# Partial sums kept in PSUM, a fifth chunk in seven products, and two output stages in seven

## The chip, the cores and the metric

One NeuronCore of a Trainium2 chip. TensorE (PE) multiplies into PSUM, VectorE (DVE) and ScalarE (ACT) read PSUM and SBUF, GpSimd (POOL) works on SBUF, SyncE (SP) issues DMAs. The metric is the device time of one execution in microseconds, here the median of three runs.

## The reference

A linear attention with 8 batches of 8 heads, 576 tokens of 64 features, followed by a feed-forward layer whose hidden value is the largest of three products.

```python
def phi(x):
    proj = np.einsum('bhsd,df->bhsf', x, w_phi)               # 64 -> 128
    proj = proj - np.max(np.abs(proj), axis=-1, keepdims=True)
    return np.concatenate([np.exp(proj), np.exp(-proj)], axis=-1)
q_p, k_p = (phi(q), phi(k))
kv = np.einsum('bhsf,bhsd->bhfd', k_p, v)
z = np.sum(k_p, axis=2)
num = np.einsum('bhsf,bhfd->bhsd', q_p, kv)
den = np.einsum('bhsf,bhf->bhs', q_p, z)[..., None] + 1e-06
x = (num / den) transposed to (batch, token, head, feature), reshaped to (4608, 512)
h = np.maximum(np.maximum(x @ w1, x @ w2), x @ w3)            # 512 -> 768
out = h @ w_out                                               # 768 -> 512
```

## The kernel before, in words

The attention is cut into 16 units `u` of four heads of one batch (`attention`). A unit loads and transposes q and k, projects both (`project`), takes maxima on DVE (`reduce`), exponentials on ACT (`k_exp`, `q_exp`), scales v on POOL, sums kv on PE, and then makes numerators: for each of its four heads PE writes two PSUM tiles of 5 x 65 columns, one for exp(proj) and one for exp(-proj) (L683); DVE scales the first into the SBUF tile `y` (L692), adds the second (L695), takes a reciprocal for two heads together (L740), and POOL multiplies it in (L741). A transposing DMA carries the result into `xT`, which holds x turned, per batch.

The feed-forward layer runs in nine chunks (`chunk`): chunks 0 to 7 are the first 512 tokens of a batch each, chunk 8 the last 64 tokens of all eight. With W2 and W3 held as differences from W1, h is W1's product plus the larger of two products clamped at zero; W1's part goes straight to the output by the product `line_w` of W1 and W_out, so that an output tile is four matmuls on x (`straight`, L924) and six on h (`down`, L929). Chunks in `SEVEN` (6, 7, 8) compute their two up products as one 2 x 2 block product with seven block multiplications in place of eight (`seven_products`): sums of quarters of x (`xs`, L799) and of the weights (`ws`, L996) are made ahead by POOL, and for each of three pairs of hidden blocks PE makes seven products of four 256-column matmuls (L820). ACT copies one of them to SBUF (L845) and DVE forms the partial sums by adding PSUM to SBUF (`joined`, L829, seven a pair); then come a relu (L862) and a maximum (L864), two of each a pair. The other chunks take 48 matmuls of 512 columns (L891), with a relu on ACT (L905) or DVE (L907) and a maximum on DVE (L901).

All of a core's work is a list of nodes. A hand-kept table, `PLAN`, gives every node its engine, its place in the order, its buffer slots and a planned start; `plan` reads it, and the instructions are written out in that order, so each engine's queue is fixed. A planned start is read only to order bank filling at the start of the kernel. `buf` and `bank` name slots shared by several tiles: eight PSUM banks, and SBUF tiles such as `raw`, `Ek0`, `Eq1`.

Of the kernel before, what the change touches and what calls it, by code (L numbers as in the profile page):

```python
# [16 lines left out]
DF = 128  # L17
DM = H * D
# [30 lines left out]
YS = 3  # L49
# [4 lines left out]
OSB = 4  # L54
EITHER = 2
SEVEN = (6, 7, 8)
# [3 lines left out]
class Buf:  # L60
# [6 lines left out]
    def __call__(self):  # L67
        if self.tile is None:
            self.tile = self.make(self)
        return self.tile  # L70

# [19 lines left out]
103G0@1.2 3A@0.7 1D@0.8 4A@1.3 10S0@0.7 12D1@4.0 11A@4.0 5D@4.2 0G@1.9 19T0@4.5 20A0@4.9 6D@4.4 29T12@5.5 32D0@6.0 9G@2.5 8G@3.2  # L91
35D@6.6 31A0@6.8 102G@3.9 260G2@4.6 16S0@1.1 104G@8.1 17G@8.3 186G3@8.6 185G@9.3 259G@10.0 1166G@10.7 13S@2.5 7A@7.2 106T3@7.4 33A0@7.5
34A@8.0 30A@8.4 107D1@8.1 119T45@8.8 122D1@9.3 187S1@2.9 124A1@9.2 123A1@9.7 112T67@9.1 115D@9.9 110T0@9.4 111A@10.2 114A@10.6
120A@11.1 121A@11.6 25T2@10.0 15D@10.5 14D@10.7 27T1@10.9 21T3@11.1 118D@10.9 26D@11.5 28D@11.8 43T04@12.2 73T21@12.3 22D@12.0
23T3@12.7 125D@12.4 113A@12.1 46D@13.0 47D0@13.3 18S1@4.3 24D@13.6 116A@12.6 76A0@13.0 45A@13.5 1169G@11.5 54A0@13.8 75A0@14.0
117A@14.4 1167G@12.2 74A@14.9 36T56@13.1 108T4@13.8 42D@14.0 39D@14.6 109D@15.2 38A@15.4 77A@15.9 41A@16.4 58A@16.8 51T37@15.1 52D@15.8
44A@17.0 126T24@15.9 130D1@16.4 105S2@5.0 131T13@16.5 333G1@13.6 129D@16.7 53D@17.0 133D@17.6 57G0@14.3 55G@14.5 2G@15.6 56G@15.8
188G@16.9 128A@17.3 37A@17.6 137A1@18.0 40A@18.2 78T0@17.5 62T47@17.8 80A@18.7 64A0@19.0 132D@18.2 48T35@18.4 50D@18.8 63D@19.4
49D@19.6 60G@17.2 61G@18.3 138G1@18.4 59G@19.5 127A@19.1 79A@19.4 68T67@19.3 134T15@19.6 263T4@19.9 190T3@20.4 135D@20.2 65T20@21.0
71A@19.7 69A@20.2 72A@20.7 70A@21.2 141A@21.6 67A@21.8 139G@20.6 334S0@8.7 142G@22.0 261G@23.1 140G@23.3 81A0@22.0 136D@20.8 191D2@21.4  # L100
264D3@22.0 192T1@21.6 85T76@22.1 86D0@22.6 66A@22.2 193A@22.3 1168G@23.5 82T05@22.4 161T3@22.7 83D@23.0 90T47@23.2 151T21@23.6
163A1@23.2 162A1@23.5 87D@23.4 93T03@23.9 265T6@24.2 84D@23.8 91D1@24.2 94D@24.6 404G0@24.2 88D0@25.1 92D@25.2 145T54@24.8 153A@24.0
155A@24.5 154A@25.0 152A@25.5 146A1@25.9 164A1@26.1 147A@26.3 194T0@25.5 1188T7@25.7 156T12@26.3 195A@26.4 144G@24.4 335G@24.6
337S0@35.1 95D@25.6 266D@26.0 1189D0@26.6 165T54@26.6 168T03@26.9 143G@24.8 166D2@27.1 169D@27.5 148T67@27.3 167D@27.9 96D1@28.4
149D@28.5 170D@28.7 189S3@36.5 1192T5@28.0 158A@26.7 403G@25.9 159A@27.2 157A@27.7 160A@28.1 262S0@42.1 150A@28.6 1190T0@28.4
1191D@29.1 171D2@29.7 1193A@28.8 89G0@26.6 332G@27.8 97G@28.6 301T46@29.0 176T31@29.3 173T27@29.6 1198T0@29.9 177D0@29.9 174D@30.2
178D@30.6 175D@31.1 179D0@31.6 304A0@29.7 305A0@30.1 302A@30.6 303A@31.1 196T53@31.3 1199A@31.6 276T21@31.6 98T7@31.9 402G@29.8
267T6@32.1 100T4@32.3 199D0@31.8 279D1@32.4 101D@33.0 268D@33.4 99D@33.6 172G1@30.6 281A0@32.0 1200T0@32.5 181T4@33.8 197A0@32.5
277A1@33.1 198A1@33.6 1201A@34.1 180G@31.9 203T67@34.2 183T5@34.5 1196T0@34.8 202D@34.0 182D@34.6 206D@35.0 406S1@42.8 338S@45.5
184D@35.6 291T45@36.2 208A@34.6 207A@35.1 278A@35.6 209D@36.0 292D0@36.6 293D@37.2 282D@37.9 204A@36.1 201A@36.6 205A@37.0 200A@37.5  # L110
1194T2@36.5 1195A@38.0 1197A@38.5 1171G@33.6 1172G@35.7 1170G@37.8 210T74@37.9 215T56@38.0 214D1@38.5 216D@38.8 280A@39.0 213D@39.4
1210T3@38.4 1173G@39.9 217D@39.7 1174G@42.0 1175G@44.1 269T20@39.3 288T45@39.5 1211A1@39.5 271A@39.9 270A@40.4 212A@40.9 273A@41.1
211A@41.6 289D@40.3 290D@40.9 274A@41.9 1206T1@40.1 1208T6@40.9 1214T3@41.8 272D@41.5 1207D@42.1 283T74@42.8 228T52@42.9 1215A@42.9
1209D@42.7 275D@43.3 287D@43.9 1204T1@43.2 230A1@43.4 229A1@43.8 1205D@44.3 1212T3@44.1 218T60@45.0 306T45@45.2 231A@44.3 285A@44.8
221A0@45.0 284A@45.2 222G0@46.5 1218T1@45.6 1213D@45.1 220D@45.7 286D@46.3 219D@46.7 1219D@47.3 309A@45.7 224A@46.1 310A@46.3 307A@46.7
294A1@47.2 308A@47.4 232A@47.9 1226T3@46.4 223G@48.5 1227D@47.9 1224T0@47.3 1225D@48.5 233T76@48.2 241A0@48.4 235A@48.7 353T15@48.5
475S1@47.7 1216T4@48.7 357D1@49.1 234A@49.2 339T23@49.6 238T0@49.9 356D0@49.4 1217D@49.8 225T57@50.5 345D@50.4 342D@51.0 236A@49.6
240A@50.2 473S1@48.4 237A@50.4 239A@50.9 346T46@51.6 227A0@51.8 226A@52.1 352D@52.0 349D@52.6 354A0@52.3 355A1@52.6 1220T0@51.9
344A@52.9 343A@53.3 296G1@50.6 242T75@52.8 341A@53.8 407S@49.8 336S2@51.9 612S0@52.5 243D1@53.3 1221D@53.7 340A@54.3 1222T1@53.1
245T37@54.0 253T02@54.9 244D@54.3 246D@54.7 297G@52.6 295G@52.8 472G3@54.8 471G@55.6 474G@56.3 1223D@55.1 254D2@55.7 247D@56.1  # L120
298T53@55.3 351A@54.8 347A@55.2 348A@55.7 350A@56.2 476S2@59.0 542G2@56.5 255D@56.5 415T10@56.5 408T74@56.7 248D1@56.9 300A1@56.7
299A@57.0 418D1@57.0 311T6@56.9 364A0@57.2 313A@57.4 314A1@57.7 312A@57.9 367A0@58.1 420A0@58.2 417A@58.7 250T23@57.1 251D@57.7
# [975 lines left out]
```

## Time and profile before

| | us |
|---|---|
| median of 3 runs | 276.3 (275.75 to 281.68) |
| the profiled execution | 276.54 |
| its span, first to last instruction | 274.7 |
| mean granted clock of TensorE | 0.993 |
| busy: PE, DVE, ACT, POOL | 265.6, 241.5, 214.2, 186.9 |
| instructions | 8748 |

The page of a profile lists busy times, the span in 40 slices with the busy share in tenths, the chain of work that ended last, and groups of instructions with their count, their total busy time and the mean time of one. Matmuls are pipelined, so their single times overlap; the step from one to the next is shorter than the mean of one.

### The profile page before, as it was taken

Reading aid. Unit: us, or ns where it says so; the run is one execution under the profiler, and the core shown is the slowest. Engines: PE = TensorE matmul, PEld = TensorE weight load, DVE = VectorE, ACT = ScalarE, POOL = GpSimd, SP = SyncE. Lnnn points to the kernel's source line nnn. Section 1 sums busy time; section 2 is a strip of 40 time slices with the busy share of each in tenths; the row PEclk is TensorE's granted clock in tenths of the full one; section 3 lists DMA queues with packets and bytes.
Section 4 is the critical chain, followed back from the end, with each engine's and each line's share of the span. In section 5 each row is a group of like instructions: output and inputs, shape, how many; then the busy total and the mean of one; then the engine's idle time right before and its main releaser. Section 6 shows DMA issues by size and latency. Waiting matters only on the chain.

```text
span 274.7 us, 8748 instructions
## 1 busy us (share of the span) xinstructions
PE 265.6 (97%) x3540; PEld 159.8 (58%) x3540; DVE 241.5 (88%) x489; ACT 214.2 (78%) x516; POOL 186.9 (68%) x183
## 2 busy tenths in 40 slices
PE   7789999999999999999999999999999999999994
PEld 4458744566565556565655455655548766686652
DVE  3799999999999888988888998999898999998871
ACT  3999999999999999779878989799987443254241
POOL 6798999999769951987569279937899856600000
PEclk9989999999999999999999999999999999999999
DMA  6999999999999999999999994596505053020253
GB/s 143 258 220 209 210 195 242 249 175 193 193 195 160 262 178 254 212 217 204 180 201 164 240 216 70 108 248 156 128 6 161 2 98 115 0 76 4 47 154 144
DMA packets 76200, 44.54 MB, mean 162 GB/s; under 512 B 52672, under 2 KB 67328, under 8 KB 76160
## 3 DMA queue, kind: packets, MB, share of 16 engines
q1 hardware_dynamic: 60880, 31.93, 53.6%
q0 software_dynamic: 14912, 11.77, 29.1%
q8 instruction: 27, 0.44, 0.6%
q10 hardware_dynamic: 368, 0.30, 0.3%
q14 instruction: 13, 0.11, 0.1%
HBM read 34.64 MB, written 9.44 MB: 160 GB/s over the span
## 4 chain that ended last, share of the span: by engine, by line
PE 89%; DVE 4%; ACT 3%; DMA 2%; issue 0%; POOLq 0%
PE ups L891 21%; PE ops L929 17%; PE ops L924 12%; PE ups L820 10%; PE psn L683 8%; PE kvps L616 7%; PE psm L642 3%; PE psq L545 3%; PE psk L545 3%; DMA qk_bf<-in_k_dram 2%; PE pm L1018 2%; ACT Eq L633 2%; DVE mk L549 2%; PE tps L508 1%; ACT Ek L553 1%; PE pst L545 1%
## 5 line engine op out<-in xcount | busy, mean ns | idle before, releaser
L633 ACT ACTIVATE Eq<-psm 128x512 bf16<-128x512 f32 (+1 forms) x160 | 81.7, 579 | 6.7 <-PE psm L642 6.1
L597 POOL TENSOR_TENSOR vab<-v_raw,em 128x1152 bf16<-128x1152 f32 (+1 forms) x36 | 68.3, 1906 | 17.5 <-ACT em L591 17.4
L553 ACT ACTIVATE Ek<-psk 128x512 bf16<-128x512 f32 x128 | 71.6, 641 | 2.2 <-DVE mk L549 1.2
L891 PE MATMUL ups<-xT,w_bf 128*128 128x512 bf16 x288 | 69.7, 380 | 0.0
L741 POOL TENSOR_TENSOR x_sb<-y,rden 128x640 bf16<-128x640 f32 x32 | 39.7, 1252 | 20.8 <-DVE rden L740 20.1
L929 PE MATMUL ops<-wout_bf,hT 128*128 128x512 bf16 (+2 forms) x222 | 52.0, 374 | 0.0
L549 DVE TENSOR_REDUCE mq<-psq 128x4 f32<-128x512 f32 x64 | 41.2, 681 | 4.8 <-PE psq L545 4.6
L549 DVE TENSOR_REDUCE mk<-psk 128x4 f32<-128x512 f32 x64 | 42.2, 681 | 2.2 <-PE psk L545 1.4
L891 PEld LDWEIGHTS <-w_bf 128*128 128x128 bf16 x288 | 25.0, 98 | 26.3 <-issue 1.3
L692 DVE TENSOR_TENSOR y<-psn,sq 128x325 f32<-128x325 f32 x64 | 30.6, 492 | 3.9 <-PE psn L683 3.1
L929 PEld LDWEIGHTS <-hT 128*128 128x128 bf16 x222 | 20.7, 98 | 21.7 <-DVE hT L864 0.5
L683 PEld LDWEIGHTS <-Eq 128*128 128x128 bf16 x640 | 26.1, 98 | 11.4 <-issue 2.3
L695 DVE TENSOR_TENSOR y<-y,psn 128x325 f32<-128x325 f32 x64 | 30.2, 487 | 2.1
L939 ACT COPY osb<-ops 128x512 f32<-128x512 f32 (+2 forms) x29 | 16.9, 582 | 17.2 <-PE ops L929 16.8
L829 DVE TENSOR_TENSOR parts<-ups,parts 128x512 f32<-128x512 f32 (+1 forms) x45 | 29.1, 679 | 1.1 <-PE ups L820 0.8
L683 PE MATMUL psn<-kv_sb,Eq 128*128 128x65 bf16 x640 | 28.7, 194 | 0.4 <-ACT Ek L553 0.4
L545 PEld LDWEIGHTS <-qkT 64*128 64x128 bf16 x576 | 18.6, 95 | 16.2 <-issue 12.3
L901 DVE TENSOR_TENSOR hT<-hT,ups 128x512 bf16<-128x512 bf16 x36 | 23.9, 676 | 2.0 <-PE ups L891 1.3
L924 PE MATMUL ops<-xT 128*128 128x512 bf16 x96 | 24.6, 381 | 0.0
L862 ACT ACTIVATE hT<-hT 128x512 bf16<-128x512 bf16 x18 | 10.8, 628 | 16.5 <-DVE hT L829 16.5
L616 PE MATMUL kvps<-vab,Ek 64*128 64x65 bf16 x1152 | 22.0, 192 | 0.0
L616 PEld LDWEIGHTS <-Ek 64*128 64x128 bf16 x1152 | 20.5, 96 | 1.0 <-issue 0.2
(84 smaller groups left out, 391.5 us busy)
## 6 DMA issues: line engine op xcount, KB each, us to landing
v_raw<-in_v_dram SPq DMA_DIRECT2D x16, 576.0 KB, 5.4
out_dram<-osb SPq DMA_DIRECT2D x31, 256.0 KB, 3.0
qk_bf<-in_k_dram POOLq DMA_DIRECT2D x15, 288.0 KB, 6.9
qk_bf<-in_q_dram POOLq DMA_DIRECT2D x15, 256.0 KB, 7.3
w_bf<-in_moe_w_dram POOLq DMA_DIRECT2D x3, 768.0 KB, 15.7
tail_raw<-in_q_dram SPq DMA_DIRECT2D x16, 64.0 KB, 4.6
out_dram<-osb SPq DMA_DIRECT2D x8, 128.0 KB, 2.3
wout_bf<-in_moe_w_out_dram POOLq DMA_DIRECT2D x1, 768.0 KB, 18.7
```

The lines of the kernel that those rows point to most:

```text
L545: nc.tensor.matmul(ps[s]()[:, i, :], lhsT=qkT()[r, n, :], rhs=wph[r, :], start=True, stop=True)
L549: return nd(kind, {"DVE": 0.598 if n == 4 else 0.331}, lambda: nc.vector.tensor_reduce(dst(m()), ps()[:, 0:n, :], AXX, ALU.max, apply_abso ...
L553: return nd("ek", {"ACT": 0.478 if n == 4 else 0.264}, lambda: nc.scalar.activation(dst(Ek[g]()), ps()[:, 0:n, :], EXP, scale=1.0 - 2.0 * ...
L597: made.append(chosen(n_, lambda n_, g=g, t0=t0, t1=t1: (nc.vector if n_.eng == "DVE" else nc.gpsimd).tensor_tensor(vab()[:, g, t0:t1, 0:D] ...
L616: nc.tensor.matmul(kvps[ab]()[:, pr, g, :], lhsT=Ek[g]()[r, t, :], rhs=vab()[r, g, t, :], start=(pr == prs[0] and g + j == 0), stop=(pr == ...
L633: return nd("eq", {"ACT": 0.478 if n == 4 else 0.264}, lambda: nc.scalar.activation(Eq[g]()[:, t0:t0 + n, :], ps()[:, 0:n, :], EXP, scale= ...
L683: nc.tensor.matmul(psn[g]()[:, i, :], lhsT=Eq[g]()[:, t, :], rhs=kv()[:, pr, ab, g, :], start=True, stop=True)
L692: n_ = nd("xu", {"DVE": 0.064 + 0.0676 * n_t}, lambda: nc.vector.tensor_tensor(yv(y()), ps(0), sq_of(sq()).unsqueeze(len(shape) - 1).to_br ...
L741: divs[pr] = nd("x", {"POOL": 1.2}, lambda pr=pr, y=y, rden=rden: nc.gpsimd.tensor_tensor(x_sb()[:, pr].rearrange("p t a d -> p a t d"), y ...
L891: nc.tensor.matmul(ups()[:, o * n:(o + 1) * n], lhsT=w_bf[i + (not plain)][:, ct, jj * P:(jj + 1) * P], rhs=tokens_of(ct)[:, cols] if halv ...
L924: nc.tensor.matmul(ops_()[:, 0:hi - lo], lhsT=tile_of(ct, tt), rhs=line_w[c_i > MOVE][:, ct, lo:hi], start=(ct == 0), stop=False)
L929: nc.tensor.matmul(ops_()[:, 0:hi - lo], lhsT=hT()[:, j, tt * P:(tt + 1) * P], rhs=wout_bf[:, j, lo:hi], start=plain and j == 0, stop=(j = ...
```

## The change

- Numerators: each head has one PSUM tile. PE writes the first five products into it, DVE scales them in place, PE adds the other five onto the result, DVE takes the reciprocal from PSUM and writes the quotient to SBUF. `y` and POOL's multiplication go.
- `seven_products`: products 1, 6, 7 and 4 of a pair accumulate in one bank (`chain`), products 5 and 3 in a second one; the bank's value is copied to SBUF between the links (`kept`), by ACT or DVE. Three sums of DVE stay a pair, the relu and the maximum of the second half become one instruction (`hp`).
- Chunk 5 joins `SEVEN`. The weight sums get a tile of their own, and one of the four overwrites half of W3's difference after the last plain chunk has read it.
- `OUT7`: in chunks 6 and 7 the output is one 2 x 2 block product in seven: x and h side by side as the left factor (five blocks of 128), `line_w` and W_out as the right one. Sums of quarters of h (`hs`) and of the two weights (`wo`) are added; 14 groups of five 256-column matmuls replace the output tiles; two stores of 256 rows replace the stores a chunk made.
- A new table orders all of it. In it chunk 8's last tile is the last work; chunk 7's split last tile is gone. `OSB`, the output tiles' slots, goes from 4 to 3.

The diff, cut to its core (`PLAN` left out):

```diff
-YS = 3
+YS = 8
-OSB = 4
+OSB = 3
-SEVEN = (6, 7, 8)
+SEVEN = (5, 6, 7, 8)
+OUT7 = (6, 7)
...
+        def numerators(pr, ab, n_sq):
+            psn = bank("psn", [P, 5, W])
+            rden = buf("rden", YS, [P, 5, 1], FP32)
+
+            def nmm(g):
+                for c in range(5):
+                    t = 8 * (c % 2) + block(2 * pr + ab, c // 2) if c < 4 else NQ + pr
+                    nc.tensor.matmul(psn()[:, c, :], lhsT=Eq[g]()[:, t, :], rhs=kv()[:, pr, ab, g, :],
+                                     start=g + c == 0, stop=True,
+                                     skip_group_check=True)
+            ready = n_kvs[pr] + eqs[pr] + eqs["t"]
+            a = nd("N", {"PE": 0.157}, lambda: nmm(0), ready, [Eq[0], kv, psn])
+            n_ = nd("xu", {"DVE": 0.41}, lambda: nc.vector.tensor_tensor(
+                psn(), psn(), sq()[:, 2 * pr + ab, :].unsqueeze(2).to_broadcast([P, 5, W]), ALU.mult), [a, n_sq], [psn, sq],
+                    locks=[psn])
+            a = nd("N", {"PE": 0.157}, lambda: nmm(1), ready + [n_], [Eq[1], kv, psn])
+            n_ = nd("xr", {"DVE": 0.1}, lambda: nc.vector.reciprocal(rden(), psn()[:, :, D:W]), [a], [psn, rden], locks=[psn])
+            return nd("x", {"DVE": 0.4}, lambda: nc.vector.tensor_tensor(
+                x_sb()[:, pr, :, ab, :], psn()[:, :, 0:D], rden().to_broadcast([P, 5, D]), ALU.mult), [n_], [psn, rden, x_sb],
+                      locks=[psn])
...
+            chain = p1[0]
+            s1 = kept(p1, 0)
+            c11 = joined(product((0, 1), lambda: w_bf[1][:, 2:4], ready + d2, []), 0, h(0), [s1], hT)
+            p6 = product(1, lambda: w_sums[1](), [s1, made[1], n_w[1][jp]], [sums_], chain)
+            u2 = kept(p6, 1)
+            p7 = product(2, lambda: w_sums[2](), [u2, made[2], n_w[2][jp]], [sums_], chain)
+            u3 = kept(p7, 0, [c11])
+            p5 = product(0, lambda: w_sums[0](), [made[0], n_w[0][jp]], [sums_])
+            c22 = joined(p5, 0, h(1), [u3], hT)
+            p4 = product((1, 1), lambda: w_sums[3](), [u3, n_w[3][jp]], [], chain)
+            second.append(ff("hp", {"DVE": 0.598}, lambda: nc.vector.scalar_tensor_tensor(
+                h(1)(), runs(chain()), 0.0, h(1)(), ALU.max, ALU.max), [p4[1], c22], [chain, hT], locks=[chain]))
+            p3 = product(3, lambda: w_bf[2][:, 2:4], [c22, made[3]] + d3, [sums_], p5[0])
+            c12 = joined(p3, 1, lambda: runs(low()), [u2, c22], part_)
+            r_ = ff("hr", {"ACT": 0.478}, lambda: nc.scalar.activation(h(0)(), h(0)(), RELU), [c11], [hT])
+            first.append(ff("hx", {"DVE": 0.35}, lambda: nc.vector.tensor_tensor(h(0)(), h(0)(), runs(low()), ALU.max),
+                            [r_, c12], [part_, hT], port=True))
...
+    def seven_outs(c_i, ready, quarter_of, hT, ff, evac, sums_, sums, made):
...
+            s_made.append(chosen(ff("hs", {"DVE": 0.5, "POOL": 1.57}, None, need, list(dict.fromkeys(used)), port=True), add))
...
+                for t in range(2):
+                    for c in range(2 + JT // 2):
+                        lhs, rhs = (x[:, c], lw[:, c]) if c < 2 else (h[:, c - 2], ow[:, c - 2])
+                        nc.tensor.matmul(ps()[:, t, :], lhsT=lhs[:, t * P:(t + 1) * P], rhs=rhs, start=first_ and t + c == 0,
+                                         stop=c == 1 + JT // 2, skip_group_check=True)
...
+        p1 = product((0, 0), plain_w(0, left), ready + lines[1] + e0, [])
+        chain = p1[0]
+        s1 = kept(p1, 0)
+        c11 = joined(product((0, 1), plain_w(1, left), ready + lines[1] + e0, []), 0, 0, left, [s1])
+        p6 = product(1, sum_w(1), [s1, made[1], s_made[1], n_ow[1]], [sums_, kept_w[1]] + hu[1], chain)
+        u2 = kept(p6, 1)
+        p7 = product(2, sum_w(2), [u2, made[2], s_made[2], n_ow[2]], [sums_, kept_w[2]] + hu[2], chain)
+        u3 = kept(p7, 0, [c11])
+        p5 = product(0, sum_w(0), [made[0], s_made[0], n_ow[0]], [sums_, kept_w[0]] + hu[0])
+        c22 = joined(p5, 0, 1, right, [u3])
+        p4 = product((1, 1), sum_w(3), e1 + ready + [u3, n_ow[3]], [kept_w[3]], chain)
...
+        p3 = product(3, plain_w(1, right), [c22, made[3], s_made[3]] + lines[1], [sums_] + hu[3], p5[0])
+        c12 = joined(p3, 1, 0, right, [u2])
...
+            s_ = ff("store", {"SP": 0.6}, None, need, [osb2[h]], xfer=[(8, 168.0, 0.6)])
...
+                    if i == 1 and SEVEN:
+                        n_w[0][j // 2].deps.append(a)
...
+        if c_i in OUT7:
+            seven_outs(c_i, ready[0], quarter_of, hT, ff, evac, sums_, sums, made)
+            return
...
-    w_tiles = [buf("w_sums", QK, [P, (1 + (BY_BATCH < UNITS)) * 2 * NB, D], BF16, of="qk_bf") for _ in range(4)]
-    w_sums = [lambda t=t: t()[:, 0:24, :].rearrange("p (c h) d -> p c (h d)", c=2) for t in w_tiles]
+    w_sum = const.tile([P, 3, 2, DFF], BF16, name="w_sum")
+    w_sums = [lambda: w_bf[2][:, 0:2]] + [lambda k=k: w_sum[:, k] for k in range(3)]
...
+            n_ow[i] = chosen(node("wo", 0, {"POOL": 2.75, "DVE": 1.0}, None, need + lines[1] + [w_nodes[3]], used, port=True), minus_ow)
```

More of the change, by code (lines that the diff above doesn't have):

```diff
@@ L95 @@
[L95 to L98, printed above, removed]
@@ L854, in pair @@
-            p5 = product(0, lambda: w_sums[0](), [made[0], n_w[0][jp]], [sums_, w_tiles[0]])
-            c22 = joined(p5, u3, low(1), one_, [c11, u2[2]])
-            v_ = part(two, 1), two_, joined(p5, u2, part(two, 1), two_)
-            p4 = product((1, 1), lambda: w_sums[3](), [n_w[3][jp]], [w_tiles[3]])
-            c21 = joined(p4, u3, own[1], hT)
-            p3 = product(3, lambda: w_bf[2][:, 2:4], [made[3]] + d3, [sums_])
-            c12 = joined(p3, v_, low(0), one_, [c11, u2[2]])
-            for i, (x, y), to in ((0, (c11, c12), first), (1, (c21, c22), second)):
-                r_ = ff("hr", {"ACT": 0.478}, lambda i=i: nc.scalar.activation(h(i)(), h(i)(), RELU), [x], [hT])
-                to.append(chosen(ff("hx", {"DVE": 0.35}, None, [r_, y], [one_, hT], port=True),
-                                 lambda n_, i=i: on[n_.eng].tensor_tensor(h(i)(), h(i)(), runs(low(i)()), ALU.max)))
+            chain = p1[0]
@@ L879, in chunk @@
         if seven:
-            evac = seven_products(c_i, ready[0], quarter_of, hT, ff)
+            evac, sums_, sums, made = seven_products(c_i, ready[0], quarter_of, hT, ff)
         for half in range(0 if seven else 1 + halves):
```

518 lines of the change are left out of this document (265 added, 253 removed).

## The prediction

> **What bounds the kernel now.** I read the page first: the busy shares, the forty slices, the chain that ended last.
>
> ```profile
> PE 265.6 (97%) x3540; PEld 159.8 (58%) x3540; DVE 241.5 (88%) x489; ACT 214.2 (78%) x516; POOL 186.9 (68%) x183
> ...
> PE   7789999999999999999999999999999999999994
> ...
> DVE  3799999999999888988888998999898999998871
> ...
> PE 89%; DVE 4%; ACT 3%; DMA 2%; issue 0%; POOLq 0%
> ```
>
> TensorE is busy nearly everywhere and holds 89% of the chain. A busy matmul row may still hide a wait, so I take its rates from the chain, where a piece ends at the start of the next one.
>
> ```profile
> 50.22 2.53 ACT Eq L633 x6
> ...
> 58.66 0.86 PE ops L924 x4
> ...
> 122.26 1.15 PE kvps L616 x72
> ...
> 124.92 1.29 PE ops L929 x6
> ...
> 134.27 0.62 PE psn L683 x20
> ...
> 240.29 4.37 PE ups L820 x40
> ...
> 249.87 0.87 PE ups L820 x8
> ...
> 269.71 0.99 PE ops L929 x6
> 270.72 0.48 ACT osb L939
> ```
>
> A matmul of 512 columns costs 1.29/6 = 0.215 us, one of 256 costs 4.37/40 = 0.109 us, a numerator matmul 0.62/20 = 0.031 us. Between 240.29 and 250.74 the pieces follow each other without a gap and all are PE's. [...]
>
> Next, the busy time by stretch; columns are PE, PEld, DVE, ACT, POOL, the granted clock, DMA.
>
> ```profile
> 10.00:30.00 20.00, 18.40 (x352) 13.24 (x350) 19.23 (x44) 19.14 (x56) 17.75 (x26) 0.91 1.22 230
> 30.00:60.00 30.00, 29.65 (x433) 16.57 (x431) 29.82 (x62) 29.94 (x77) 29.20 (x20) 1.00 1.15 217
> ...
> 180.00:190.00 10.00, 10.00 (x109) 5.39 (x111) 9.40 (x18) 9.61 (x24) 6.11 (x4) 1.00 0.99 253
> 190.00:200.00 10.00, 10.00 (x159) 5.82 (x152) 8.89 (x21) 9.74 (x27) 7.64 (x5) 1.00 0.41 89
> 200.00:212.00 12.00, 12.00 (x258) 7.84 (x257) 10.47 (x23) 9.54 (x26) 11.92 (x10) 1.00 0.35 91
> ...
> 225.00:240.00 15.00, 14.89 (x101) 9.53 (x100) 14.69 (x27) 4.33 (x8) 9.16 (x9) 1.00 0.26 75
> 240.00:250.00 10.00, 10.00 (x81) 7.71 (x80) 10.00 (x18) 4.87 (x9) 0.00 (x0) 1.00 0.15 55
> ...
> 270.00:274.70 4.70, 0.69 (x5) 0.20 (x2) 0.00 (x0) 0.48 (x1) 0.00 (x0) 0.95 0.32 113
> ```
>
> Three things are to be seen. Up to 60 us, DVE, ACT and POOL are all full, and PE is fed by them. From 60 to 270 us PE is full, and in 225 to 250 it stays full although DVE has no slack at all (24.69 of 25 us). After the last matmul (269.71 + 0.99 = 270.70) come 4.0 us of copy and store. So PE work taken away after 60 us is worth its full length, as long as DVE and ACT keep up; and 180 to 212, with DVE at 28.76 and ACT at 28.89 of 32 us, is where they have little to give.
>
> **The change, part by part.** The sum is made against the profiled execution: 276.54 us, of which 274.7 are span. The median shown is 276.3, 0.2 lower.
>
> *Chunk 5 in seven products.* Its up stage was 2 x 6 x 4 = 48 matmuls of 512 (48 x 0.215 = 10.3 us) and becomes 3 x 7 x 4 = 84 of 256 (9.2 us): -1.1 us of PE. *Outputs of chunks 6 and 7.* Each was 4 x (4 + 6) = 40 matmuls of 512, 8.6 us (chunk 7's split tile has the same columns), and becomes 7 x 2 x 5 = 70 of 256, 7.65 us: -1.0 each. *Numerators.* Still 640 matmuls, in groups of 5 in place of 10: nothing, with ends of -0.3 and +1 us for twice as many handovers. PE in all: **-3.1 us**.
>
> DVE and ACT come next; the groups of instructions, and some of DVE's timeline for start-to-start times:
>
> ```profile
> L597 POOL TENSOR_TENSOR vab<-v_raw,em 128x1152 bf16<-128x1152 f32 x28 | 59.1, 2121 | 16.7 <-ACT em L591 16.7
> ...
> L741 POOL TENSOR_TENSOR x_sb<-y,rden 128x640 bf16<-128x640 f32 x32 | 39.7, 1252 | 20.8 <-DVE rden L740 20.1 <-POOL vab L597 0.6
> L692 DVE TENSOR_TENSOR y<-psn,sq 128x325 f32<-128x325 f32 x64 | 30.6, 492 | 3.9 <-PE psn L683 3.1 <-POOL x_sb L741 0.4
> L695 DVE TENSOR_TENSOR y<-y,psn 128x325 f32<-128x325 f32 x64 | 30.2, 487 | 2.1
> ...
> L864 DVE TENSOR_TENSOR hT<-hT,parts 128x512 bf16<-128x512 bf16 x18 | 8.4, 492 | 0.2
> ...
> L996 POOL TENSOR_TENSOR w_sums<-w_bf,w_sums 128x512 bf16<-128x512 bf16 x6 | 6.9, 1153 | 0.0
> ...
> L740 DVE RECIPROCAL rden<-y 128x10 f32<-128x10 f32 x32 | 6.5, 207 | 0.1
> ...
> L845 ACT COPY parts<-ups 128x512 f32<-128x512 f32 x9 | 5.1, 587 | 6.8 <-DVE hT L829 3.8 <-PE ups L820 1.4 <-DVE hT L864 0.8
> ```
>
> ```profile
> 211.15 0.49 DVE L692 TENSOR_TENSOR y<-psn,sq 128x325 f32<-128x325 f32 x1
> 211.56 0.48 DVE L695 TENSOR_TENSOR y<-y,psn 128x325 f32<-128x325 f32 x1
> ...
> 212.37 0.20 DVE L740 RECIPROCAL rden<-y 128x10 f32<-128x10 f32 x1
> 212.49 0.84 DVE L695 TENSOR_TENSOR y<-y,psn 128x325 f32<-128x325 f32 x2
> ...
> 225.14 1.89 DVE L829 TENSOR_TENSOR parts<-ups,parts 128x512 f32<-128x512 f32 x3
> ```
>
> A 325-column operation takes its place for 0.41 us (211.15 to 211.56), a reciprocal for 0.12, a 512-column sum from PSUM for about 0.62 (1.89 less the last one's run-out, over three).
>
> *Numerators on DVE.* Per unit before: 4 x (0.41 + 0.41) + 2 x 0.12 = 3.5 us. After: scaling in place, reciprocal and division, 4 x (0.41 + 0.12 + 0.41) = 3.8. No row shows a DVE write into PSUM, nor a 5-column reciprocal from it. I bound the three operations by half and by twice the nearest rows (-1.9 and +3.8 us a unit) and take the rows themselves: +0.3 us a unit. [...]
>
> The division leaves POOL: 32 x 1252 ns. Its waits say what that is worth:
>
> ```profile
> POOL x_sb L741 <- DVE rden L740: 20.1, 10, 9.1
> POOL vab L597 <- ACT em L591: 17.4, 8, 6.9
> ```
>
> POOL waits for ACT and DVE for longer than it makes them wait (0.4 us, in L692's row), so its 40 us buy nothing on the path after 60 us. Before that POOL is full too, but there the chain runs over ACT's exponentials (50.22). I take 0 for the reordered start, with ends of -1.5 and +1.5: between 10 and 60 us DVE and ACT have 1 us of idle each to win, POOL 3.
>
> *The seven products themselves.* Per pair, DVE's 7 sums and 2 maxima become 4 and 1; ACT's copies go from 1 to 3 and its relus from 2 to 1. For chunks 6, 7 and 8 that is 9 x (3 x 0.62 + 0.41) = 20 us less DVE, in a stretch where PE was not waiting for DVE: cover, worth nothing itself. Chunk 5 goes the other way, in 180 to 212: DVE +12 x 0.62 + 3 x 0.41 - 6 x 0.62 = +4.9, ACT 9 copies and 3 relus for 6 relus, +6 x 0.59 = +3.5, with three units' numerators +0.9. DVE and ACT together then want 57.65 + 9.3 = 67 of 64 us, and either can take the copies: 3 us over, 1.5 on each. What is late next is the last attention units and, behind them, PE. **+1.5 us**; ends 0 (that work slips behind 212, where DVE has been relieved) and +3.
>
> *Added waits.* The second half of a numerator is queued on PE behind DVE's scaling, and products 6, 7 and 4 behind the copy of their bank. PE runs its queue in order, so all that is written behind them waits too. I counted the new table's order at the rates above: between the two halves of a numerator stand 0.78 us of other PE work at the least and 1.8 in the median, between the links of a chain 1.03 at the least. The scaling takes 0.49. Covered: 0, if DVE comes to it at once. The in-place difference of W3's first half runs on POOL after chunk 4's last products; at 1.15 us each the three are done ahead of chunk 5's fifth product in that order. The half-width sums of hT and the four of W_out (768 columns, 1.5 times 492 ns or 1153 ns) stand between chunks whose products fill PE: 0.
>
> *The end.* Chunk 8's last tile now closes the kernel instead of chunk 7's split one.
>
> ```profile
> L939 ACT COPY osb<-ops 128x512 f32<-128x512 f32 x27 | 16.1, 597 | 14.9 <-PE ops L929 14.4 <-ACT sq L661 0.4
> ...
> 258.23 11.58 SPq L943 DMA_DIRECT2D out_dram<-osb  x12
> ...
> out_dram<-osb SPq DMA_DIRECT2D x8, 128.0 KB, 2.3
> ...
> out_dram<-osb ACTq DMA_DIRECT2D x1, 192.0 KB, 2.2
> ```
>
> Its copy takes 0.60 in place of 0.48, and it has two stores of SP (at most 11.58/12 = 0.97 us to issue) that land in 2.3, in place of one of 2.2: **+0.8 us**, ends +0.2 and +1.2.
>
> Sum: 276.54 - 3.1 + 1.5 + 0.8 = 275.7, and 0.2 less for the median: **275.5 us**.
>
> **Rivals.** (a) *The whole saving arrives*: chunk 5's extra work slips behind 212 and the start gains: 276.3 - 3.1 + 0.3 - 1 = 272.5. For it: PE full at 225 to 250 beside a full DVE. Against: DVE and ACT counted above. (b) *The numerator's round trip is not covered.* In 30 to 60 us DVE had 0.18 us idle, and a scaling that stands behind a 0.6 us reduction reaches PE 1.1 us or more after the first half, over the least cover. With 64 round trips, 0.1 us uncovered in the mean is 6.4 us, 275.5 + 6.4 = 281.9, just slower by 2%; that is the point from which it decides. For it: DVE at 88%. Against: median cover of 1.8. (c) *PE is not the bound and nothing is gained*: the new table is bound by DVE and ACT throughout as before 60 us; 276.3, the end's 0.8 and 1 us of handovers give 278.1.
>
> **Chances.** Forecast (one to two microseconds off): 0.55. (a) 0.18, (c) 0.19, (b) 0.08. Within 2% is 270.8 to 281.8, about what a measurement of this kernel can tell from no change, and the three runs before already spread to 281.68; forecast, (a) and (c) lie inside. Past it on the fast side needs over 1.5 us beyond (a): 0.05. Slower: (b) and a little of (c): 0.09. Range: 272.3 from (a), 279.5 from (c) and part of (b).
>
> **What would show it.** Right: some 3600 matmuls; PE full from 60 us to its end near 269; DVE slack behind 215 us; DVE and ACT full in 180 to 212 with a PE loss of one to two microseconds there; POOL near 150 us. Wrong by (b): idle of PE before the numerator's second matmuls, ended by DVE's scaling. Wrong by the operations' prices: scaling, reciprocal or division far from 0.49, 0.21, 0.49 us in their rows. Wrong by the start: the first output matmul moved by over 2 us from 58.66.

## The result, and the profile after

The changed kernel takes 278.96 us (278.88 to 279.28), the kernel before 276.21 on the same chip: 1.0108 times as long [1.0088, 1.0127]. The forecast was 275.5 within 272.3 to 279.5. The time lies in that range and within the 2% that had most of the chance, but on the other side of the kernel before: a gain of 0.8 us was expected, a loss of 2.8 came. The profiled execution took 279.28 us, of which 277.5 are span.

The page of the changed kernel: busy times, two rows of slices, the chain by engine, and the rows of the numerators' operations.

```profile
PE 264.6 (95%) x3601; PEld 170.0 (61%) x3636; DVE 241.0 (87%) x514; ACT 215.2 (78%) x521; POOL 164.8 (59%) x166
...
PE   7989999999999999999899999999999999999993
...
DVE  2898899999999798999878798999999899998850
...
PE 84%; DMA 2%; DVE 2%; issue 1%; ACT 0%; DVEq 0%; ACTq 0%
...
L702 DVE TENSOR_TENSOR psn<-psn,sq 128x325 f32<-128x325 f32 x64 | 30.4, 494 | 3.7 <-PE psn L697 2.3
L707 DVE TENSOR_TENSOR x_sb<-psn,rden 128x320 bf16<-128x320 f32 x64 | 29.0, 477 | 0.3
```

PE's busy time fell by 1.0 us only, and the chain is still PE's. (Of the 3636 matmuls, one to each weight load, 35 have no record in this trace, so the row is a little low.) A PE row that reads "full" again hides what happened. So I counted the matmuls of each line in each stretch, took them at the rates of the prediction (0.215, 0.109, 0.031 us and so on), and subtracted that work from the stretch's length. What is left is time that PE lost, busy or not; it is good to about half a microsecond.

| stretch (us) | lost before | lost after | difference |
|---|---|---|---|
| 0 to 60 | 20.3 | 20.1 | -0.2 |
| 60 to 120 | 2.5 | 3.0 | +0.5 |
| 120 to 180 | 2.3 | 5.0 | +2.7 |
| 180 to 215 | 1.0 | 2.9 | +1.9 |
| 215 to 270 | 0.3 | 0.7 | +0.4 |
| 270 to the end | 4.3 | 5.1 | +0.8 |

PE's work at those rates fell from 244.0 to 240.7 us, by 3.3, about the saving that was forecast. The losses rose from 30.6 to 36.8. But for the rounding, that is the +2.8 by which the spans differ.

Three kinds of loss stand out in the trace. First, the chain of the changed kernel at 134 us and at 240 us:

```profile
134.48 0.25 PE psn L697 x8
134.73 0.99 issue
135.72 0.23 PE psn L697 x2
...
240.55 0.45 PE ups L791 x4
...
241.03 1.12 DVE sums L767
242.15 0.43 DVE osb L887
...
244.00 3.05 PE ups L791 x25
```

At 134.73 PE waits for nothing the profile names, for 0.99 us. The page has 28 instruction packets on q8 (0.46 MB, 16 KB each) for PE's 3636 weight loads and as many matmuls (that q8 is PE's queue is inferred), so a packet is a block of some 260 instructions. The next block's packet began at 133.33 and landed at 134.22. The instruction 260 places ahead of the stall ran at 127.5; if the block was asked for then, which is an estimate, its packet began 5.8 us late. Meanwhile three loads of k were under way that the new table issues back to back; that they held the block up is inferred.

```profile
125.39 2.20 POOL L459 DMA_DIRECT2D qk_bf<-in_k_dram  x3
```

The windows beside it (columns as before; the last two are the DMA share and GB/s):

```profile
128.00:130.00 2.00, 1.95 (x68) 1.44 (x62) 1.91 (x5) 1.71 (x5) 0.00 (x0) 1.00 1.39 154
130.00:132.00 2.00, 2.00 (x24) 0.99 (x23) 2.00 (x4) 2.00 (x7) 0.00 (x0) 1.00 1.45 138
...
134.00:136.00 2.00, 1.01 (x14) 0.56 (x12) 1.72 (x5) 1.95 (x4) 2.00 (x2) 1.00 0.41 66
```

The second is at 241. The chain leaves PE for DVE, whose timeline, with POOL's beside it, shows why:

```profile
232.60 0.56 DVE L853 TENSOR_TENSOR h_sums<-hT 128x768 bf16<-128x768 bf16 x1
...
234.72 0.41 DVE L767 TENSOR_TENSOR sums<-xT 128x512 bf16<-128x512 bf16 x1
235.05 0.55 DVE L853 TENSOR_TENSOR h_sums<-hT 128x768 bf16<-128x768 bf16 x1
...
236.71 1.42 DVE L853 TENSOR_TENSOR h_sums<-hT,h_sums 128x768 bf16<-128x768 bf16 x1
...
239.36 1.50 DVE L1095 TENSOR_TENSOR ow_sums<-wout_bf,ow_sums 128x768 bf16<-128x768 bf16 x1
240.78 1.37 DVE L767 TENSOR_TENSOR sums<-xT 128x512 bf16<-128x512 bf16 x1
```

```profile
236.57 1.15 POOL L767 TENSOR_TENSOR sums<-xT 128x512 bf16<-128x512 bf16 x1
...
239.11 1.33 POOL L767 TENSOR_TENSOR sums<-xT 128x512 bf16<-128x512 bf16 x1
240.52 1.35 POOL L767 TENSOR_TENSOR sums<-sums,xT 128x512 bf16<-128x512 bf16 x1
```

A sum of 768 columns that takes DVE 0.56 us alone (at 232.60) takes 1.42 to 1.50 where POOL runs sums all the while, and one of 512 columns 1.37 in place of 0.41; POOL's own take 1.15 where DVE runs none (at 226.42), and 1.33 and 1.35 in the last rows above. So sums of two SBUF operands on the two engines lengthen each other here, and the rows give the price.

The third is spread out. In 180 to 212 PE, DVE and ACT are all full:

```profile
180.00:190.00 10.00, 9.88 (x191) 7.50 (x191) 9.64 (x20) 9.67 (x25) 8.66 (x8) 1.00 0.95 165
190.00:200.00 10.00, 9.95 (x172) 7.58 (x172) 9.98 (x23) 10.00 (x26) 6.63 (x5) 1.00 0.05 18
200.00:212.00 12.00, 11.75 (x190) 6.96 (x191) 11.94 (x28) 12.00 (x34) 5.26 (x6) 1.00 0.72 193
```

But PE's waits there are short, and a piece of chunk 5 is dearer behind a projection than behind a numerator:

```profile
188.07 0.15 PE psn L697 x5
188.23 0.44 PE ups L791 x4
...
190.64 0.32 PE psm L659 x2
190.96 0.54 PE ups L791 x4
191.51 0.11 PE psm L667
```

The projections (L659) work on 64 rows of the array, products and numerators on 128 (`64*128` and `128*128` in their rows of the trace). The new table cuts PE's queue into smaller pieces, and by the records of the weight loads PE changes between the two 126 times in place of 110. Up to 60 us there are 40 in place of 46, from 60 to 215 us 82 in place of 64, and 4 behind 215, where there were none.

From 60 us to the end the profile names four waits of PE; the kernel before has none there.

```profile
PE psn L697 <- issue: 1.0, 1, 1.0
PE ups L791 <- DVE hT L809: 0.6, 1, 0.6
PE ups L940 <- DMA xT<-x_sb: 0.3, 1, 0.3
PE ups L940 <- DVE osb L993: 0.2, 1, 0.2
```

The first two are the places above, at 134 and 243 us. The last two are at 159 and 161: x came late through a transposing DMA, and the copy of an output tile was late because it stood behind a store (DVE waited 1.3 us for it). From start to start of the matmuls these two cost 0.8 us.

### The profile page after: what moved, and what is told of

Same layout as the page of the kernel before. It is cut to its first block, busy times and chain, and to the rows that moved or that the text cites. A ratio compares the mean times of both kernels' runs of the same rounds, so it can differ in the third digit from the quotient of the medians.

```text
span 277.5 us, 8932 instructions
## 1 busy us (share of the span) xinstructions
PE 264.6 (95%) x3601; PEld 170.0 (61%) x3636; DVE 241.0 (87%) x514; ACT 215.2 (78%) x521; POOL 164.8 (59%) x166
## 4 chain that ended last, share of the span: by engine, by line
PE 84%; DMA 2%; DVE 2%; issue 1%; ACT 0%; DVEq 0%; ACTq 0%
PE ups L940 18%; PE ups L791 13%; PE ops L983 12%; PE ops L978 8%; PE psn L697 8%; PE kvps L633 7%; PE ops L876 5%; PE psm L659 3%; PE psq L562 3%; PE psk L562 2%; DMA out_dram<-osb 2%; PE pm L1071 2%; PE pst L562 1%; PE pwT L1061 1%; PE tps L525 1%
## 5 line engine op out<-in xcount | busy, mean ns | idle before, releaser
L940 PE MATMUL ups<-xT,w_bf 128*128 128x512 bf16 x227 | 57.5, 380 | 1.1 <-DMA xT<-x_sb 0.3
L983 PE MATMUL ops<-wout_bf,hT 128*128 128x512 bf16 x162 | 39.6, 379 | 0.3
L940 PEld LDWEIGHTS <-w_bf 128*128 128x128 bf16 x240 | 20.9, 98 | 23.0 <-issue 2.2
L702 DVE TENSOR_TENSOR psn<-psn,sq 128x325 f32<-128x325 f32 x64 | 30.4, 494 | 3.7 <-PE psn L697 2.3
L707 DVE TENSOR_TENSOR x_sb<-psn,rden 128x320 bf16<-128x320 f32 x64 | 29.0, 477 | 0.3
L799 ACT COPY parts<-ups 128x512 f32<-128x512 f32 x31 | 18.1, 614 | 11.5 <-PE ups L791 8.4
L983 PEld LDWEIGHTS <-hT 128*128 128x128 bf16 x168 | 15.1, 98 | 16.4 <-issue 0.3
L993 ACT COPY osb<-ops 128x512 f32<-128x512 f32 x23 | 14.0, 609 | 14.0 <-PE ops L983 13.6
L950 DVE TENSOR_TENSOR hT<-hT,ups 128x512 bf16<-128x512 bf16 x30 | 20.3, 679 | 2.9 <-PE ups L940 2.6
L791 PEld LDWEIGHTS <-w_bf 128*128 128x128 bf16 x192 | 18.2, 98 | 3.5 <-DVE hT L809 0.9
L809 DVE TENSOR_TENSOR hT<-ups,parts 128x512 bf16<-128x512 f32 x24 | 15.6, 680 | 0.8 <-PE ups L791 0.8
```

The lines of the kernel that those rows point to most:

```text
L702: n_ = nd("xu", {"DVE": 0.41}, lambda: nc.vector.tensor_tensor(psn(), psn(), sq()[:, 2 * pr + ab, :].unsqueeze(2).to_broadcast([P, 5, W]), ...
L791: nc.tensor.matmul(ps()[:, o, :].rearrange("p (b t) -> p b t", t=m.shape[-1]) if len(m.shape) == 4 else ps()[:, o, :], lhsT=weight()[:, c, ...
L940: nc.tensor.matmul(ups()[:, o * n:(o + 1) * n], lhsT=w_bf[i + (not plain)][:, ct, jj * P:(jj + 1) * P], rhs=tokens_of(ct)[:, cols] if halv ...
L983: nc.tensor.matmul(ops_()[:, 0:hi - lo], lhsT=hT()[:, j, tt * P:(tt + 1) * P], rhs=wout_bf[:, j, lo:hi], start=plain and j == 0, stop=(j = ...
```

## The experiments

Eighteen kernels ran. Theory A is that of the prediction: the loss in 180 to 215 comes from DVE and ACT. Against it stood a store wait, the collision of DVE and POOL, the instruction blocks, the loads, and the changes of rows. Numbers in an edit are nodes of the table, T, D, A, G and S its engines PE, DVE, ACT, POOL and SP.

**Four output slots again.**

```diff
-YS = 8
+YS = 6
-OSB = 3
+OSB = 4
```

> The changed kernel with four osb buffers again in place of three (slots dealt out anew, nothing else moved; wphi_f takes the place of one of them at the start, and rden has six buffers for eight, both for room in SBUF). Theory 'three buffers': the copy of an output tile at 160.0 us waited 1.34 us for the store before last, whose issue stood behind a transposing DMA of SP; with a fourth buffer that wait goes, and about 0.9 us with it: 278.1 us, ratio to the changed kernel 0.997. Rival 'no cost': PE had other work to catch up, the wait moves: 279.0. Both expect the two stretches in which PE waits for nothing that the profile shows (0.55 us at 28.7, 0.99 us at 134.7) to stay, since PE's instructions are the same.

279.65 us, 1.0141 [1.0102, 1.0181]. DVE no longer waits for a store, but PE gets other waits:

```profile
PE psk L562 <- DMA qkT<-qk_bf: 1.7, 1, 1.7
...
PE ups L940 <- DMA xT<-x_sb: 0.8, 1, 0.8
```

This profile is of the slowest of six executions (281.67 us). The smaller `OSB` is not the cause of the loss: with the slot back nothing is gained. That the edit made the new waits isn't shown.

**DVE relieved, twice.** Theory A was put to the test by leaving work out: the scaling of units 4 to 15 (48 DVE operations), and, by itself, chunk 5's relu and maxima.

```diff
-            n_ = nd("xu", {"DVE": 0.41}, lambda: nc.vector.tensor_tensor(
+            n_ = nd("xu", {"DVE": 0.41}, lambda: u >= 4 or nc.vector.tensor_tensor(
...
-            second.append(ff("hp", {"DVE": 0.598}, lambda: nc.vector.scalar_tensor_tensor(
+            second.append(ff("hp", {"DVE": 0.598}, lambda: c_i == 5 or nc.vector.scalar_tensor_tensor(
```

> The changed kernel with the scaling of the numerators left out for units 4 to 15 (their outputs lack that factor): 48 DVE operations of 0.41 us, 20 us of DVE, and with them the wait of each second half for DVE. Theory 'DVE over-full, handovers': of the 9 us of PE time that are lost between 60 and 215 us in the changed kernel (5.9 before), 2 to 4 come back: 275 to 277 us, ratio to the changed kernel 0.985 to 0.993. Rival 'ACT or the loads bind there': under 0.7 us: 278.5 to 279.

> The changed kernel with chunk 5's relu and both its maxima left out (9 operations, 3.0 us of DVE and 1.6 of ACT at 185 to 205 us; chunk 5's output is not maxed). By the forecast's step the stretch of 180 to 212 us asks DVE and ACT for more than they have, 1.5 us on each; without 3.0 and 1.6 of it PE gets back 1 to 2 us: 277.2 to 278.2. Rival: PE's loss there has another cause, 279.2.

279.89 us, 1.013 [1.0093, 1.0168], and 278.95, 1.0094 [1.0062, 1.0127]. The first leaves the wait of each numerator's second half out as well. Neither gains. The same stretches without chunk 5's relu and maxima:

```profile
190.00:200.00 10.00, 10.00 (x177) 7.70 (x175) 8.96 (x21) 9.86 (x26) 6.62 (x5) 1.00 0.07 23
200.00:212.00 12.00, 12.00 (x193) 6.94 (x190) 10.76 (x25) 11.19 (x32) 5.33 (x6) 1.00 0.75 193
```

DVE has 1.0 and 1.2 us to spare, ACT 0.8 in the second, and PE still loses 2.9 us in 180 to 215 (2.3 with the scaling left out). Theory A falls: a full DVE was not what PE paid for. ACT was relieved less, by 1.0 us in 180 to 212, but the list of PE's waits above has none in 180 to 215, for either engine.

**The collision, moved and then removed.** First the last W_out sum went to POOL; then it stayed on DVE, ahead of chunk 6's relu work, and the x sum went to POOL.

```diff
 # first: PLAN
-D: 1605 1271 1694 1609 ... 1645
+D: 1605 1609 ... 1645 1694
-G: 1691 1613
+G: 1691 1271 1613
 # second: PLAN
-D: 1599 1612 ... 1605 1271 1694 1609
+D: 1599 1271 1612 ... 1605 1609
-G: 1695 1665
+G: 1695 1694 1665
```

> The changed kernel with two DVE operations taken out of the way of POOL's at 238 to 243 us: the last W_out sum (512 + 768 columns) goes to POOL, into its idle time before 235 us, and the sum of x for chunk 8 that DVE makes comes after POOL's. Theory 'DVE and POOL hold each other up on SBUF operands': these took 1.50 and 1.37 us on DVE beside POOL's sums where 0.56 and 0.41 were to be expected; the work behind them comes 1 us earlier, 0.6 us of PE's idle at 243 goes, and the kernel takes 278.0 us (0.9965). Rival 'DVE is late anyway there': the PSUM copies behind them are paced by PE, 279.0 (1.000).

> The changed kernel with the last W_out sum still on DVE but 4 us earlier, ahead of POOL's run of sums for chunks 7 and 8, and the x sum of chunk 8 that DVE made beside it at the end of POOL's run. Theory 'held up on SBUF operands' (in the first edit of this place the wait at 243 us went, 0.9 us, and one of 1.3 us came at 232, where POOL's part then met DVE's maxima): no DVE operation over 1.2 us is left in 230 to 245, and the time is 0.9 us less than the unaltered changed kernel, 278.3 us. Rival: DVE is behind there by as much anyway, 279.2.

The first: 279.88 us, 1.0148 [1.0101, 1.0196]. DVE's maxima met POOL's moved sum instead (timelines of DVE and of POOL, then PE's wait behind it):

```profile
231.67 3.31 DVE L828 TENSOR_TENSOR hT<-hT,parts 128x512 bf16<-128x512 bf16 x3
```

```profile
232.55 1.81 POOL L1095 TENSOR_TENSOR ow_sums<-wout_bf,ow_sums 128x768 bf16<-128x768 bf16 x1
```

```profile
PE ops L876 <- DVE hT L828: 1.3, 1, 1.3
```

The second: 277.99 us, 1.0065 [1.0042, 1.0088], 1.0 less than the changed kernel, where 0.9 was expected. The sum is back at its own price, and PE is full:

```profile
234.84 0.55 DVE L1095 TENSOR_TENSOR ow_sums<-wout_bf,ow_sums 128x768 bf16<-128x768 bf16 x1
...
237.31 1.44 DVE L853 TENSOR_TENSOR h_sums<-hT,h_sums 128x768 bf16<-128x768 bf16 x1
```

```profile
240.00:250.00 10.00, 10.00 (x94) 8.95 (x93) 8.53 (x15) 5.83 (x11) 4.29 (x4) 1.00 0.40 159
```

So this collision costs about 1 us, by the times and by the wait at 243 us, which is gone. The expectation that no operation of DVE over 1.2 us would be left was missed: one of 1.44 still stands beside a sum of POOL. This is the best version of the change, still slower than the kernel before.

**The price of a change of rows.** Eighteen small matmuls were put ahead of the first products of chunks 7 and 8, where all is 128 rows: once on 64 rows, once on 128. Their result is not used.

```diff
+                    [nc.tensor.matmul(ps()[:, 0, 0:64], lhsT=weight()[r, 0, 0:P], rhs=idle[r, 0:64], start=True, stop=True)
+                     for r in ((slice(0, 64),) if first_ and c_i in (7, 8) else ())]   # the other: slice(0, 128)
```

> The changed kernel with 18 more matmuls in chunks 7 and 8 (235 to 262 us, where PE is full and no attention runs), one ahead of each new bank of up products, on 64 rows and 64 columns; the product behind each overwrites what it wrote. Theory 'changing between 64 and 128 rows costs PE about 0.1 us each way': 18 x (0.03 + 2 x 0.096) = 4.0 us more than the changed kernel, 283.2 us, and 3.5 us more than the run with 128 rows. Rival 'only the columns count': 18 x 0.03 = 0.5 us more, as with 128 rows.

> The same 18 matmuls on all 128 rows, 64 columns: the control. By both theories 18 x 0.03 = 0.5 us more than the changed kernel, 279.7 us.

283.05 and 279.61 us: 3.44 apart, 0.095 us for each of 36 changes. The chains, 64 rows first:

```profile
254.05 0.13 PE ups L787
254.18 0.54 PE ups L791 x4
```

```profile
249.44 0.03 PE ups L787
249.47 0.44 PE ups L791 x4
```

The same matmul costs 0.10 more, and so do the four behind it: both ways are paid. The 0.54 is the piece behind the projection above. The runs show this price, 0.095 us a change, and not what it comes from.

The mixed stretches show the same price. From 180 to 215 us, from start to start of the matmuls, the steps at a change of rows come 0.09 to 0.10 us late in both kernels: 14 of them before, 1.3 us, and 24 in the changed kernel, 2.3 us. That is 1.0 more, of the 1.9 in the table. But for those with a missing record, only one step there is late by over 0.1 us for another reason: 0.13 at 181 us, behind a maximum of DVE.

**Fewer changes.** On top of the best version, twelve pieces of PE's queue (not some 30) were moved by up to 0.9 us. The expectation counts 142 changes and 118 left, because it takes every product of L667 for one on 64 rows; by the trace 10 of the changed kernel's 16 work on 128. The traces have 126 changes and 116: ten went, not 24, worth 0.95 us by the price above.

```diff
 # PLAN, two of twelve moves
-T: 1048 1482 1058 ... 1079 1112
+T: 1482 1048 1058 ... 1079 1537 1112
```

> The kernel of the run ports2 (278.0 us) with some 30 pieces of PE's order moved by at most 0.9 us between 60 and 215 us, so that products on 64 rows (projections, K's sums) stand next to one another: 24 changes between 64 and 128 rows fewer of 142; no work is added or left out. Theory 'changes cost 0.095 us each in the mixed stretches too': 24 x 0.095 = 2.3 us less, 275.7 us, ratio to the kernel before 0.999; if some of the moved pieces then wait for a bank or an operand, half of that, 276.9. Rival 'the loss there is something else': 278.0 (1.0065), or more by the new waits.

283.63 us, 1.0279 [1.025, 1.0308]: 5.6 us slower than without it. PE got new waits for DVE and ACT, transposes and stores came late on SP's queue, and what the changes saved was lost several times over:

```profile
PE psk L562 <- DVE mq L566: 1.0, 2, 0.5
PE psq L562 <- DVE mq L566: 0.5, 1, 0.5
PE psq L562 <- ACT Ek L570: 0.5, 1, 0.5
```

The price of a change is shown by the pair above, and it stands in the trace of the mixed stretches; no run shows it coming back, as the one that took changes out brought other waits.

**Loads and instruction blocks.** Each of the kernel's 52 idling matmuls of 256 columns (L1139) was cut into three of 84: 104 matmuls more, so that by the count above every later block of PE's instructions ends at another piece of work.

```diff
-            nc.tensor.matmul(idler[:, 0:2 * P], lhsT=idle, rhs=idle.unsqueeze(1).to_broadcast([P, 2, P]), start=True, stop=True)
+            [nc.tensor.matmul(idler[:, 0:84], lhsT=idle, rhs=idle[:, 0:84], start=True, stop=True) for _ in range(3)]
```

> The changed kernel with each idler matmul of 256 columns split into three of 84, so that PE's instructions behind them are some 104 matmuls further on in the stream; the work is the same. Theory 'instruction pages': PE's instructions come in blocks of 16 KB (256 instructions, 128 matmuls with their weight loads) over the same DMA engines as the data; a fetch that was late (start 26.97 and 133.33 us) made PE wait 0.55 us at 28.7 and 0.99 us at 134.7. The block ends fall elsewhere, and both waits go: 277.5 us (0.9945). Rival 'the numerators': what stands there waits for something else in the kernel, and both waits stay at the same matmuls: 279.0 (1.000).

279.49 us, 1.0117 [1.0086, 1.0148]: no gain, but the stall near 29 us moved into another piece, which speaks for the block and against the work:

```profile
30.73 0.40 PE kvps L633 x18
31.13 0.70 issue
31.83 0.46 PE kvps L633 x18
```

This edit, the four slots and the first collision edit in one kernel:

> The changed kernel with the edits of all three of the other runs. If their gains are separate losses on one path, they add up: 0.9 + 1.0 + 1.5 = 3.4 us, 275.6 us, ratio to the changed kernel 0.988 and just under the kernel before. Rival 'one hides the other' (DVE and ACT have no slack in 180 to 212 us, so that what comes earlier waits there): 277 us or more.

280.96 us, 1.0156 [1.012, 1.0192]: they do not add to a gain. The unaltered kernel once more, and beside it POOL's first loads ahead of a copy, and later the loads of k spread out:

```diff
 # start: PLAN
-G: 108 2 9 272 17
+G: 9 272 108 2 17
 # loads: PLAN (and two more loads of k in the same way)
-G: 716 676 ... 677 937 1011 864 ... 748 936 865
+G: 716 937 676 ... 677 864 ... 748 863 865
```

> The changed kernel, not altered: the reference for the other runs of this call. If its first runs (278.9 to 279.3 us) were typical, 279.1 us. If it is right that the start hangs on when the first tail of Q lands (POOL waited 4.6 us for it ahead of its first Q loads; in the runs of the three edits PE waited 2 us for it that it had not waited in the first profile), then this kernel spreads as they did: 279.0 to 281, by what happens before 25 us and in 150 to 180 us.

> The changed kernel with four loads (both Q loads of unit 0, that of unit 1, the K load of unit 3) on POOL ahead of the copy of the first tail, as they stood before the change; nothing else is moved. Theory 'the loads stand behind a wait': they are issued at 2.7 us in place of 7.8, unit 0's Q lands earlier, and 1.2 to 1.5 us of what the start lost against the kernel before comes back: ratio to the unaltered changed kernel 0.995. Rival 'bandwidth': at 2 to 6 us DMA is busy with the K loads and tails anyway, the tail lands later by as much as Q lands earlier: 1.000.

> The changed kernel with three pairs of loads on POOL put elsewhere: K of unit 12 before the products of unit 8 (some 10 us earlier), K of unit 13 some 16 us later, and the Q loads of units 11 and 12 exchanged, so that loads come in the order in which SP's transposing DMAs need them, and no three K loads (864 KB) are issued within 2.2 us. Theory 'bunched loads': these filled the DMA engines at 126 to 134 us, held up PE's instruction block (5.7 us late, 1.0 us lost at 134.7) and let SP wait for Q of unit 11 at 153 to 156.5 us with stores and transposed outputs behind it (1.34 + 0.34 us of waits); without them the time is 1.5 to 2 us less, ratio to the unaltered kernel 0.994. Rival 'DMA is full anyway': total bytes are the same, and the waits come at other places: 1.000.

Unaltered: 279.25 us (278.12 to 280.23); in its profile, of an execution of 278.35, the stall at 134 us is absent, and 120 to 180 loses 3.5 us in place of 5.0. So this stall isn't part of every execution. Loads at the start: 279.33, 1.0112 [1.0089, 1.0136], nothing. Loads of k: 278.89, 1.0104 [1.0082, 1.0126], no difference that can be told from the unaltered kernel.

**The parts of the change alone.** The new numerators in the kernel before, in an order of my own (the second half at least 1.02 us of PE work behind the first, the edit is `numerators` of the diff with a table for it):

> The kernel before with the new numerators alone: chunks, loads and the order of all else are the old ones; the second half of each numerator stands behind at least 1.02 us of other PE work, as in the changed kernel, with reciprocal and division right behind it on DVE. By the forecast's step (0.3 us more of DVE a unit, handovers covered, POOL's 40 us worth nothing) the time stays at 276.2 us, ratio 1.000. Rival 'handovers cost': DVE comes late to the scaling and PE waits behind it, or the longer hold of the PSUM bank delays the next product; 64 round trips at 0.03 to 0.1 us give 278 to 282 (1.007 to 1.023), and the numerators are what the change loses on between 60 and 215 us.

317.28 us, 1.1467 [1.1432, 1.1502]. The waits:

```profile
DVE rden L688 <- PE psn L679: 31.7, 45, 1.6
...
PE psn L679 <- DVE psn L684: 9.0, 13, 1.7
```

Here DVE stood between a scaling and a reciprocal with nothing else in its queue; 41 us over 64 numerators is 0.65 each, if all of it is theirs. In the changed kernel's order PE waits for a scaling nowhere behind 60 us, by the list of its waits, and without the scaling of units 4 to 15 nothing was gained. Rival (b) is thus real, and it is the order that keeps it away.

Chunk 5 plain again, in two orders:

```diff
-SEVEN = (5, 6, 7, 8)
+SEVEN = (6, 7, 8)
```

> The changed kernel with chunk 5 again in plain products (48 matmuls of 512 columns, a relu and a maximum for each pair of tiles), at the places of the seven; the nine differences of W3's and W2's parts that it must not overtake come behind its products. One part undone. PE's work grows by 1.1 us, DVE's falls by 4.9 and ACT's by 3.5. By the forecast's step (1.1 gained, 1.5 lost to DVE and ACT being over-full in 180 to 212 us) it takes 0.4 us less, 278.7; by the loss that the profile shows there (3.1 us of PE time in place of 0.85) 1.1 less, 278.0. Rival 'PE bounds there': 1.1 us more, 280.2.

> The kernel of the run ports2 (278.0 us) with chunk 5 in plain products again; the nine differences of weights that it must not overtake are made by DVE right behind each pair's products, in place of POOL ahead of them. PE's work grows by 1.1 us, its changes between 64 and 128 rows fall with the number of products (84 matmuls in 21 groups become 48 in 12). By the forecast's step 0.4 us less, 277.6; if the changes of rows took back chunk 5's saving, it is worth nothing: 278.0 give or take 0.4; if PE's work alone counts, 1.1 more, 279.1.

285.13 us, 1.0329 [1.0308, 1.035], and 289.42, 1.0467 [1.0411, 1.0524]. In the first, POOL's weight differences stood ahead of the last units' products; in the second, PE waited 3.4 us for DVE's quotients.

The last three chunks of the change behind the attention of before, first with POOL's W_out sums ahead of the last divisions, then behind them:

```diff
 # before.py with seven_products and seven_outs of the change, and
+OUT7 = (6, 7)
 # its table up to the last units, then the changed one's nodes of chunks 6 to 8
```

> One part alone: the kernel before up to its last attention units, with its numerators, loads and plain chunk 5, and from there the changed kernel's chunks 6, 7 and 8 (sums in PSUM, outputs of 6 and 7 in seven products, in the order of the run ports2), begun at the same distance from the last unit, give or take 0.5 us. By the forecast's steps the two outputs save 2.0 us of PE, in a stretch in which DVE has been relieved, and the end costs 0.4 to 0.8: 276.0 - 2.0 + 0.6 = 274.6, ratio to the kernel before 0.995. Rival 'the new sums cost as much as the products save': 276.0 or more.

> As ffn (the kernel before up to its last units, then the changed kernel's chunks 6, 7 and 8), with chunk 6's sums of x where the kernel before has them, two sums of W_out on POOL behind the last division of unit 15 and one on DVE, and the chunks begun 0.5 us later. By the forecast's steps 276.0 - 2.0 + 0.6 = 274.6 us, ratio to the kernel before 0.995. Rival 'the new sums cost as much as the products save': 276.0 or more. If POOL, which must divide for the last units and make 2.8 us sums of W_out in the same stretch, is late again, PE's waits name it, and the run tells that the outputs need the numerators' new form to free POOL.

290.22 us, 1.0512 [1.0452, 1.0572], and 282.37, 1.0215 [1.0185, 1.0245]. In the second PE still waited 3.9 us for DVE at L866, because the last unit's division on POOL came late. All four orders made waits of their own, so these runs say nothing on what a part is worth.

## Why the prediction was wrong, step by step

*PE's saving*, -3.1: right, -3.3 by the count. *The end*, +0.8: right, +0.8, and the last copy took 0.59 where 0.60 was expected. *The operations' prices* held: scaling 0.494 and division 0.477 in the rows above; some 3600 matmuls were 3636.

*DVE and ACT in 180 to 212*, +1.5: the stretch lost 1.9 more, but not for the reason given. Two kernels with some of that work left out lost 2.9 and 2.3 there all the same, so "3 us over" was a count of busy time and no wait. What PE is seen to pay there is changes of rows: 10 more lie in this stretch, 1.0 us. The other 0.9 has no wait in the trace, and each of the two counts is good to half a microsecond only. That the stretch lost about what was forecast is luck. The prediction took PE's rates from chains of one kind and priced no change between kinds; that is the first step that failed, a term at 0 where, behind 60 us, 22 x 0.095 = 2.1 us stand.

*The sums of hT and W_out*, 0: wrong, about 1 us. I let POOL's and DVE's sums lie side by side; DVE's row for 768 columns was worked out as 1.5 times 492 ns, and beside POOL it is 1.42 to 1.50 us. The second step that failed is "between chunks whose products fill PE": they didn't fill it while DVE was held.

*The reordered start*, 0 within 1.5: it came out at -0.2. My own test for it, the first output matmul, moved by 3.6 us (58.66 to 55.06) with no gain or loss, so the test was poor. What the new table moved between 120 and 180 us I didn't price at all: it lost 1.2 to 2.7 more there by the profiles. In the larger, 0.99 is the instruction block, 0.8 the waits at 159 and 161 us, and 0.4 to 0.5 changes of rows, which are in the 2.1 above.

The sum now, for the profiled execution: 276.5 - 3.3 + 0.8 - 0.2 = 273.8; +2.1 for changes of rows, +1 for the collision, +1.0 for the instruction block, +0.8 for the two waits: 278.7 of 279.28. The price of a change and the collision have runs of their own; the block and the two waits are read off one trace, and no experiment took them out alone. They differ from execution to execution (the unaltered kernel's other profile has no stall at 134 us), so what they cost in the median stays open. Rival (c) gave the nearest time, 278.1, but its reason, that PE isn't the bound, is not what the runs show: PE holds 84% of the chain and paid for each loss. POOL's forecast, near 150 us, was wrong as well: 164.8, because the new sums are its work.

## What to carry to other kernels

When an engine is full, count its work at its own rates and look at what is left of each stretch: the busy row can't tell a cheaper program from one that stalls while busy (PE's fell by 1.0 us here, its work by 3.3). Price what a finer order costs besides its instructions: changes of rows on TensorE (0.095 us each here) and sums of VectorE beside sums of GpSimd (up to 0.96 us more for one here). To learn whether a full engine is the bound, leave some of its work out before reasoning on its share.

## What the runs showed of the hardware

A change between 64 and 128 rows costs PE 0.095 us each way (283.05 against 279.61 us for 36 changes). A VectorE sum of two SBUF operands beside a GpSimd one takes up to 0.96 us longer (1.37 in place of 0.41 for 512 columns, 1.50 in place of 0.56 for 768). PE lost 0.99 us at 134.73, and by an estimate a block of its instructions had come late: its packet ran from 133.33 to 134.22 us, 5.8 us late if it was asked for when the instruction some 260 places ahead ran, at 127.5. Three loads of k were under way; that they held it up is inferred. With 28 such packets in the trace, PE is seen to stall so at two places, at 28.67 (0.55 us) and at 134.73 (0.99).
